# Two channels in one Toeplitz matmul, and filter rows loaded in pieces on 13, 11 or 9 DMA engines

## The chip, the core and the metric

The kernel runs on one core of one Trainium2 chip. The metric is the device time of one execution in microseconds; the time of before is the median of three runs, and one further execution was profiled.

## What is computed

Two independent blocks, whose outputs are put side by side (512 columns each, 2048 positions, bf16).

```python
# block A: attention, 32 heads of 16
qkv = (x @ wqkv).reshape(B, S, 3, H, Dh).transpose(2, 0, 3, 1, 4)
p = softmax(einsum("bhqd,bhkd->bhqk", q, k) * Dh ** -0.5)
a = einsum("bhqk,bhkd->bhqd", p, v).transpose(0, 2, 1, 3).reshape(B, S, D) @ wo
# block B: gated long convolution, 512 channels
k_shift = sum(k shifted by t * shift_k[:, ks - 1 - t])      # 4 taps
kv = k_shift * v
y = irfft(rfft(kv, 2S) * rfft(ssm_k, 2S))[:S] + kv * ssm_D  # causal convolution over 2048 positions
b = q * y
out = concatenate([a, b], -1)
```

## The kernel before

All five engines run instruction lists that are written out in full when the program is built. A planner in the kernel keeps a modelled time for each engine (`Eng.op`, `Tensor.op`, `dma`) and places each piece of work into the list with it, so a change of any cost constant moves instructions everywhere.

**Attention.** There are 2048 blocks of 128 keys x 512 queries for one head. A step T (`emit_qk`, L681) multiplies two to four blocks (`qk_mm`, L728) into PSUM banks 0 to 5. ACT exponentiates most of them, two or three banks an instruction (`emit_exp`, L761). One block of some steps goes to DVE, which needs four instructions for it (`exp_on_dve`, L803, L810 twice, L815). Two steps later PE multiplies the results with V (`emit_pv`, L844). Projections of later head groups, the product with `wo` and the multiplies of the convolution's input are "units" (`pe_unit`, L438; `unit_step`, L1088) that are put between steps by due times (`jobs`, L1065). `warm_up` (L1202, matmuls at L1219) fills idle time of PE with matmuls by zeros.

**Convolution.** It runs on PE between the steps. For each channel the reversed filter row, with 128 zeros behind it, is stored in an HBM scratch `kz` (L553). A load (`load_wr`, L990) reads it 128 times, each partition shifted by one element: a Toeplitz matrix of 128 x 2048 in the ring `WR`. `WR` holds 16 rows: four slots of four channels; the last slot first holds parts of v (`VST`, L282). `conv_lags` (L1003) multiplies for each of 16 lags n and four channels c: weights are the input `KV[:, qd, n:16, c]` (128 positions x up to 16 blocks of positions, one block a column), the moving side is 128 columns of `WR`, and the four channels write four 32-row strips of PSUM bank 7. After four such groups (16 channels) DVE copies the bank to one half of `YB` (L1028), and after eight `conv_turn` (L1033) transposes eight 128x128 tiles back and DVE multiplies them into `QN`, which holds q (L1048). `KV` is written by DVE at L514, from the shift's matmuls (L468) times v. From step N_OPEN on the convolution runs (`emit_bg`, L1143): it takes up to seven lags between steps (`LAGS`), if the rows are expected to be there (`h_wr` + WAIT), if there is room before the next exponential, and if PE's instruction fetch is expected to keep up.

**Instruction fetch in the planner.** `Tensor.op` (L182) counts two instruction words for each matmul, in blocks of 256. Crossing into a block starts a fetch of the next that is taken to land FETCH (L108, 6.3 us) later; `spare` (L204) says how many words may still be issued, and `emit_bg` (L1169) and `warm_up` (L1215) keep to it.

**Queues.** Filter rows go out on SP's queue, each group of four loads waiting for the last matmul that read its slot. POOL's queue carries the copies into `QT` (L499), the loads and stores of `QN` (L1000, L1052), and the stores of `OUTA` (L966). POOL starts with memsets (L392 to L403) and builds diagonal matrices of the taps (L560).

Of the kernel before, what the change touches and what calls it, by code (L numbers as in the profile page):

```python
# [9 lines left out]
U16 = mybir.dt.uint16  # L10

# [13 lines left out]
NB = S // 128  # L25
PAD = 128
# [3 lines left out]
R_W = 16  # L30
# [6 lines left out]
N_OPEN = 66  # L37
# [34 lines left out]
PLAN = 710  # L72
# [13 lines left out]
DMA_KB = 394  # L86
X_KB = 200
WINDOW = 3.4
HALF = 0.25
TURN = 0.2  # L90
# [17 lines left out]
FETCH = 6.3  # L108
# [111 lines left out]
def bass_concat_heads__mha_block__ssm_conv_h3__prompt_kernel(  # L220
# [36 lines left out]
    KV = sb("KV", [128, C // 4, NB, 4])  # L257
# [143 lines left out]
    h_va1 = pool.op(lambda e: e.memset(VA[:, :, :, 8 * VW:VROW].rearrange("p s k e -> p (s k) e"), 1.0))  # L401
    h_qt0 = pool.op(lambda e: e.memset(QT[:, 1:R_Q, :, :].rearrange("p r n f -> p (r n f)"), 0.0), us=(1.5, 1.6))
# [87 lines left out]
    def evac_unit(u, bank, h):  # L490
# [18 lines left out]
        elif kind == "kv":  # L509
            _, c, i = u  # L510
            dst = KV[:, 32 * c:32 * c + 32, NB - 4 - 4 * i:NB - 4 * i, :]
            val = VST[c][:, NB - 4 - 4 * i:NB - 4 * i, :].rearrange("p b (k c) -> p k b c", c=4)
            src = PS[:, bank, :].rearrange("p (b k c) -> p k b c", b=4, c=4)
            h_kvc[c] = hh = urgent(lambda e: e.tensor_tensor(dst, src, val, ALU.mult), [h, h_vn[c]], us=V512)  # L514
# [470 lines left out]
    h_yb = [None]  # L985
# [4 lines left out]
    def load_wr():  # L990
        while wr_free and wr_next[0] < C // 4:
            (i, dep), qd = wr_free.pop(0), wr_next[0]
            wr_next[0] += 1
            wr_slot[qd] = i
            for c in range(4):
                src = bass.AP(tensor=kz_ap.tensor, offset=kz_ap[4 * qd + c, 0].offset, ap=[[1, 128], [1, S]])
                h_wr[qd] = dma(sp, d_wr[i], WR[:, 4 * i + c, :], src, [h_kzw[0], dep])
# [4 lines left out]

    def conv_lags(qd, n0, n1):  # L1003
        kk = qd % 8
        deps = [h_wr[qd], h_kvc[qd // 32]]
        r = 4 * wr_slot[qd]
        if kk % 4 == 0 and n0 == 0:
            deps.append(bank_free[BGB])

        def fn(e):  # L1010
            ins = None
            for n in range(n0, n1):
                for c in range(4):
                    ins = e.matmul(PS[32 * c:32 * c + NB - n, BGB, 128 * (kk % 4):128 * (kk % 4) + 128],  # L1014
                                   lhsT=KV[:, qd, n:NB, c],
                                   rhs=WR[:, r + c, 128 * (NB - 1 - n):128 * (NB - n)],
                                   start=(n == 0), stop=(n == NB - 1), tile_position=(0, 32 * c))
            return ins
        h = pe.op(fn, deps, run=LAG * (n1 - n0), kind="C", lat=0.4)
        if n1 == NB:  # L1020
            wr_free.append((wr_slot[qd], h))
            load_wr()
            if kk % 4 == 3:
                half = kk // 4
# [4 lines left out]
                            [h, h_yb[0]], slack=S_C, us=V512)  # L1029
# [3 lines left out]
    def conv_turn(b, bank):  # L1033
        pbf = PS[:, bank, :].bitcast(BF16)

        def fn(e):
            ins = None
            for k in range(8):
                ins = e.transpose(pbf[:, 128 * k:128 * k + 128], YB[:, k // 4, 128 * (k % 4):128 * (k % 4) + 128],
                                  IDN[:, :])  # L1040
            return ins
        h = pe.op(fn, [bank_free[bank], h_ybw[0], h_idn], run=0.445, kind="F")
        h_yb[0] = h
        sl = b // 8
        yv = pbf.rearrange("p (c j) -> p c j", j=32)[:, :, 0:NB].rearrange("p c j -> p j c")
        yv = bass.AP(tensor=yv.tensor, offset=pbf[:, NB - 1:NB].offset, ap=[yv.ap[0], [-1, NB], [32, CHB]])
        qv = QN[:, :, CHB * (b % 8):CHB * (b % 8) + CHB]
# [11 lines left out]
    units = [("kv", c, i) for c in range(2) for i in range(4)] + [(x, 1, i) for i in range(4) for x in "kv"]  # L1059
# [7 lines left out]
    jobs += [(step(9 + 7 * c) - 8, ("kv", c + 2, i)) for c in range(2) for i in range(4)]  # L1067
    jobs += [(step(25 + 2 * qb) + 8 * t, ("op", qb, t)) for qb in range(NQB - 1) for t in range(4)]
    jobs.sort(key=lambda j: j[0])
    state = {"qd": 0, "lag": 0, "turn": False, "started": False, "lags": 0.0, "left": C // 4 * NB, "t": 0.0}  # L1070
# [6 lines left out]
    def next_unit(T):  # L1077
        if T < N_OPEN:
            return early[0] if early and ready(early[0][1]) else None
        if state["turn"]:  # L1080
            return T, ("turn", state["qd"] // 8 - 1)
# [6 lines left out]
    def unit_step(T):  # L1088
# [7 lines left out]
        while not tight:  # L1096
# [23 lines left out]
            us = pe.turn("F") + (0.445 if u[0] == "turn" else 0.478 if u[0] in ("kv", "v") else 2 * MM) + SWITCH  # L1120
# [22 lines left out]
    def emit_bg(T):  # L1143
# [5 lines left out]
        if T - end[0] in tail_mm:  # L1149
            assert st["qd"] == C // 4 and not st["turn"], (T, st)  # L1150
# [3 lines left out]
        if st["qd"] == C // 4 and not st["turn"]:  # L1154
# [3 lines left out]
        if st["turn"] and st["qd"] == C // 4:  # L1158
# [11 lines left out]
        while left > 0 and st["qd"] < wr_next[0] and kv_n[st["qd"] // 32] == 4 and at(h_wr[st["qd"]]) + WAIT <= pe.t:  # L1170
            if st["turn"] and st["qd"] % 4 == 3 and st["lag"] + left >= NB:
                left = NB - 1 - st["lag"]
                if left <= 0:
                    break
# [3 lines left out]
            n1 = min(n0 + left, NB)  # L1178
# [4 lines left out]
            st["lag"] = n1 % NB  # L1183
            if n1 == NB:
                st["qd"] += 1
                if st["qd"] % 4 == 0:
                    st["turn"] = st["turn"] or st["qd"] % 8 == 0
                    break

    def filler_place(limit):  # L1190
# [5 lines left out]
        if state["started"] and state["lag"]:  # L1196
            return BGB, 0, NB, 128 * (state["qd"] % 4), 1, False
# [53 lines left out]
    assert state["qd"] == C // 4 and not state["turn"] and not jobs and not part[0], (state, jobs)  # L1251
# [65 lines left out]
```

## Time and profile before

| | |
|---|---|
| runs shown | 826.47 us median (825.16, 826.47, 830.9) |
| the profiled execution | 828.52 us, its span 826.8 us |
| PE clock granted, mean | 0.996 |
| first and last convolution matmul starts | 89.7 and 804.1 us |
| filter loads | 512 of 512 KB, 8.4 us from issue to landing (median) |
| DMA packets | 109235, 291.41 MB, mean 352 GB/s |
| ACT busy by windows | 99.4% from 100 to 200 us, 96.8% from 200 to 300, 99.3% from 300 to 400, 99.9% or more from 400 to 700 |
| DMA engines' busy share | 0.98 to 1.03 from 100 to 780 us |

Busy time is the time in which an engine had at least one instruction in execution; ACT's instructions overlap at their ends, so their mean duration times their number is more than the busy time. The chain of waits gives ACT's exponentials (L761) 77.2% of the span, four DVE lines 10%, PE lines 9%. POOL and SP have nothing on it after the first 11 us. A row of a group reads: line, engine, operation, output <- inputs, shapes, count, then busy us, mean ns, and the engine's idle time ahead of it with what ended it.

### The profile page before, as it was taken

The numbers are of one execution on the slowest core, as the hardware profiler recorded it, in microseconds if no ns is written. First come the engines' busy times: TensorE is split into PE (matmuls) and PEld (weight loads), VectorE is DVE, ScalarE is ACT, GpSimd is POOL, SyncE is SP. The second block draws the span as 40 slices with busy tenths as digits, with TensorE's granted clock in tenths as the row PEclk, the third lists the DMA queues.
The fourth block names the chain that finished last, engine by engine and source line by source line (L and its number), as shares of the span: only waits on it lengthen the run. The fifth ranks groups of instructions, "written<-read, shape, count | busy, mean of one in ns | idle before, by whom it ended". The sixth has DMA issues, their size and how long they took to land.

```text
span 826.8 us, 30549 instructions
## 1 busy us (share of the span) xinstructions
PE 762.2 (92%) x13603; PEld 324.2 (39%) x13642; DVE 794.2 (96%) x1360; ACT 807.0 (98%) x727; POOL 78.7 (10%) x155
## 2 busy tenths in 40 slices
PE   8998989999999899999899999999999999998987
PEld 3343434443333344444333344444433333333332
DVE  4999999999999899999999999999999999999985
ACT  6999999999999899999999999999999999999987
POOL 3300320010100101001011010101002002010000
PEclk9999999999999999999999999999999999999999
DMA  9998499999999999999999899999999999999922
GB/s 220 233 300 304 151 382 404 385 379 407 393 407 405 394 401 389 405 354 367 394 388 391 318 372 383 394 408 387 408 407 352 378 393 362 399 382 367 375 83 77
DMA packets 109235, 291.41 MB, mean 352 GB/s; under 512 B 37680, under 2 KB 41648, under 8 KB 108720
## 3 DMA queue, kind: packets, MB, share of 16 engines
q1 hardware_dynamic: 102256, 280.80, 90.8%
q0 software_dynamic: 5648, 8.27, 3.1%
q8 instruction: 108, 1.77, 0.9%
q10 hardware_dynamic: 1200, 0.39, 0.2%
q14 instruction: 23, 0.19, 0.1%
HBM read 276.83 MB, written 6.42 MB: 343 GB/s over the span
## 4 chain that ended last, share of the span: by engine, by line
ACT 77%; DVE 10%; PE 9%; issue 2%; DMA 1%; SPq 0%
ACT PT L761 77%; DVE EH L810 4%; PE PS L728 3%; DVE FX L803 2%; PE PS L1014 2%; PE PS L844 2%; DVE PTD L815 2%; PE PS L1219 1%; PE PS L468 1%; DMA xT<-in_A_x_dram 1%; DVE DT L905 0%; DVE YB L1028 0%; SPq L312 0%; DVE KV L514 0%; DVE OTN L925 0%
## 5 line engine op out<-in xcount | busy, mean ns | idle before, releaser
L761 ACT ACTIVATE PT<-PS 128x1024 bf16<-128x1024 f32 (+2 forms) x722 | 804.1, 1376 | 8.8 <-PE PS L728 8.3
L728 PE MATMUL PS<-QT,KTo 32*128 32x512 bf16 x2048 | 287.1, 385 | 38.7 <-ACT PT L761 14.1
L844 PE MATMUL PS<-PT,VA 128*32 128x512 bf16 x1771 | 199.7, 391 | 6.6 <-issue 3.5
L1014 PE MATMUL PS<-WR,KV 128*12 128x128 bf16 (+15 forms) x8192 | 201.6, 220 | 4.4 <-issue 4.3
L803 DVE TENSOR_SCALAR FX<-PS 128x512 f32<-128x512 f32 x277 | 187.9, 682 | 8.3 <-PE PS L728 8.0
L815 DVE SCALAR_TENSOR_TENSOR PTD<-EH,FX 128x512 uint16<-128x512 f32 x277 | 185.7, 677 | 0.0
L810 DVE SCALAR_TENSOR_TENSOR EH<-EH 128x512 f32<-128x512 f32 x277 | 185.4, 680 | 0.0
L810 DVE SCALAR_TENSOR_TENSOR EH<-FX 128x512 f32<-128x512 uint16 x277 | 184.5, 682 | 0.1
L1014 PEld LDWEIGHTS PS<-WR,KV 128*12 128x12 bf16 (+15 forms) x8192 | 140.6, 88 | 71.9 <-issue 42.5
L728 PEld LDWEIGHTS PS<-QT,KTo 32*128 32x128 bf16 x2048 | 73.3, 91 | 237.8 <-ACT PT L761 178.9
L1219 PE MATMUL PS<-IDN,ZW 128*32 128x512 bf16 (+3 forms) x498 | 132.2, 334 | 0.0
L312 POOL DMA_DIRECT2D QT<-QS x120 | 59.2, 501 | 483.7 <-DVE DR L912 133.7
L844 PEld LDWEIGHTS PS<-PT,VA 128*32 128x32 bf16 x1771 | 48.0, 93 | 114.0 <-issue 97.5
L844 PE MATMUL PS<-PTD,VA 128*32 128x512 bf16 x277 | 83.1, 383 | 0.0
L1219 PEld LDWEIGHTS PS<-IDN,ZW 128*32 128x32 bf16 x498 | 41.8, 96 | 24.1 <-issue 10.4
L905 DVE STREAM_TRANSPOSE DT<-PS 128x512 f32<-128x512 f32 x32 | 22.7, 709 | 7.3 <-PE PS L844 6.8
L1028 DVE CAST YB<-PS 128x512 bf16<-128x512 f32 x32 | 21.9, 684 | 1.4 <-PE PS L1219 1.1
L844 PEld LDWEIGHTS PS<-PTD,VA 128*32 128x32 bf16 x277 | 20.4, 95 | 1.6 <-DVE PTD L815 0.2
L955 PE MATMUL PS<-WKV,OTN 128*128 128x512 bf16 x53 | 16.9, 383 | 2.1 <-issue 1.6
L479 PE MATMUL PS<-WKV,xT 128*128 128x128 bf16 x256 | 18.1, 220 | 0.1
L456 PE MATMUL PS<-xT,WKV 128*128 128x512 bf16 (+1 forms) x52 | 15.0, 373 | 2.9 <-issue 1.1
L447 PE MATMUL PS<-xT,WQ 128*128 128x512 bf16 x45 | 14.4, 382 | 2.4 <-issue 2.1
(65 smaller groups left out, 209.2 us busy)
## 6 DMA issues: line engine op xcount, KB each, us to landing
WR<-kz_scratch SPq DMA_DIRECT2D x512, 512.0 KB, 8.4
kz_scratch<-WR SPq DMA_DIRECT2D x1, 2176.0 KB, 8.3
QN<-in_B_q_dram POOLq DMA_DIRECT2D x2, 1024.0 KB, 12.4
out_dram<-QN POOLq DMA_DIRECT2D x2, 1024.0 KB, 8.6
QT<-QS POOLq DMA_DIRECT2D x120, 16.0 KB, 5.3
out_dram<-OUTA POOLq DMA_DIRECT2D x12, 128.0 KB, 5.2
QN<-in_B_ssm_k_dram SPq DMA_DIRECT2D x1, 1024.0 KB, 8.3
OTN<-in_B_ssm_k_dram SPq DMA_DIRECT2D x1, 1024.0 KB, 9.2
```

Of the source, the lines that this page charges most:

```text
L312: f(outp, inp).then_inc(dsem.sem, 16)
L479: ins = e.matmul(PS[:, bank, 128 * j:128 * j + 128], lhsT=xT[:, dc, (4 * sc + j) * 128:(4 * sc + j + 1) * 128], rhs=WV[:, dc, o * 128:(o + ...
L728: ins = e.matmul(PS[:, bank, :], lhsT=KTo[32 * s:32 * s + 32, OF[n_] % 2, kt * 128:(kt + 1) * 128], rhs=QT[32 * s:32 * s + 32, n_ // 2 % R ...
L761: h_exp[T] = act.op(lambda e: e.activation(PT[:, p0:p0 + n, :].rearrange("p b f -> p (b f)"), PS[:, banks[0]:banks[0] + n, :].rearrange("p ...
L803: h_f = urgent(lambda e: e.tensor_scalar(fx, PS[:, bank, :], FIX_ADD, FIX_HI, ALU.add, ALU.min), [h, h_last.get(i - R_FX)], slack=S_FX)
L810: st["h"] = dve.op(lambda e: e.scalar_tensor_tensor(eh, src, (P1, P2)[j], src, ALU.add, ALU.mult), [st["h"], h_last.get(i - R_EH)], us=us)
L815: lambda e: e.scalar_tensor_tensor(out16, eh, P3, fx, ALU.mult, ALU.add),
L844: ins = e.matmul(dst, lhsT=w, rhs=rhs, start=(k == 0), stop=(k == KT - 1), tile_position=(0, 32 * s))
L905: h_t = urgent(lambda e: e.transpose(out=dt, in_=PS[:, PVB, :]), [h, h_mul.get(n - 1)], slack=S_T, us=(0.63, 0.751))
L1014: ins = e.matmul(PS[32 * c:32 * c + NB - n, BGB, 128 * (kk % 4):128 * (kk % 4) + 128], lhsT=KV[:, qd, n:NB, c], rhs=WR[:, r + c, 128 * (NB ...
L1028: hh = urgent(lambda e: e.tensor_copy(YB[:, half, :].rearrange("p (k i) -> p k i", k=4), src), [h, h_yb[0]], slack=S_C, us=V512)
L1219: pe.op(lambda e, s=s, k=k, rhs=rhs, bank=bank, rows=rows, c0=c0, first=first: e.matmul(PS[32 * s:32 * s + rows, bank, c0:c0 + 128 * k], l ...
```

## The change

The convolution is cut otherwise. Filters are loaded as Toeplitz matrices of 64 partitions instead of 128, and two channels lie above each other in the 128 partitions. The input `KV` becomes twice as large, [128, 64, 2, 32, 4]: blocks of 64 positions, where the column of an upper channel has zeros in the lower half and the other way round. POOL sets it to zero once. A group `qd` is eight channels, there are 64 groups, and 32 lags of 64 positions instead of 16 of 128; the number of matmuls is the same, 8192, with 2 to 32 weight columns. Lag -1 is a half step with 64 moving columns. One `conv_turn` is due after four groups, with four transposes instead of eight.

Rows: each half's 64 shifted rows of four channels come in two DMAs, of 52 and 12, then 55 and 9, then 63 and 1 rows; the division changes at groups 21 and 43. By the change's name these run on 13, 11 and 9 of the 16 DMA engines. `WR` has three slots of four rows instead of four. The multiplies of chunk 1 of `KV` become units behind the start of the convolution, and N_OPEN goes from 66 to 64. The planner's constants for the plan's length (710 to 705), for turns (0.2 to 0.05) and for the instruction fetch (6.3 to 5.5 us) change, and the rates of the row loads are given (260 and 215 KB/us).

```diff
-R_W = 16
+R_W = 12
-N_OPEN = 66
+N_OPEN = 64
+KV1 = 2
-PLAN = 710
+PLAN = 705
+PARTS = [(52, 12), (55, 9), (63, 1)]
+PHASE = [21, 43]
+RATES = [260, 215]
-TURN = 0.2
+TURN = 0.05
-FETCH = 6.3
+FETCH = 5.5
...
-    KV = sb("KV", [128, C // 4, NB, 4])
+    KV = sb("KV", [128, C // 8, 2, 2 * NB, 4])
...
+    h_kv0 = pool.op(lambda e: e.memset(KV[:, :, :, :, :].rearrange("p o r u g -> p (o r u g)").bitcast(U32), 0), us=(8.8, 8.9))
     h_qt0 = pool.op(lambda e: e.memset(QT[:, 1:R_Q, :, :].rearrange("p r n f -> p (r n f)"), 0.0), us=(1.5, 1.6))
...
-            h_kvc[c] = hh = urgent(lambda e: e.tensor_tensor(dst, src, val, ALU.mult), [h, h_vn[c]], us=V512)
+            for half in range(2):
+                for ch in range(2):
+                    hs, cs = slice(64 * half, 64 * half + 64), slice(64 * ch, 64 * ch + 64)
+                    dst = KV[cs, 16 * c:16 * c + 16, 1 - half, q0 + ch:q0 + 8:2, :].rearrange("p o q g -> p q o g")
+                    h_kvc[c] = hh = (dve.op if half or ch else urgent)(
+                        lambda e, dst=dst, hs=hs, ch=ch: e.tensor_tensor(dst, src[hs, :, ch], val[hs, :, ch], ALU.mult),
+                        [h, h_vn[c], h_kv0], us=(0.335, 0.46))
...
-            for c in range(4):
-                src = bass.AP(tensor=kz_ap.tensor, offset=kz_ap[4 * qd + c, 0].offset, ap=[[1, 128], [1, S]])
-                h_wr[qd] = dma(sp, d_wr[i], WR[:, 4 * i + c, :], src, [h_kzw[0], dep])
+            parts = PARTS[sum(qd >= q for q in PHASE)]
+            for ch in range(2):
+                p0 = 0
+                for n in parts:
+                    row = 128 * (qd // 16) + 64 * ch + 4 * (qd % 16)
+                    src = bass.AP(tensor=kz_ap.tensor, offset=kz_ap[row, p0].offset, ap=[[1, n], [LKZ, 4], [1, S]])
+                    h_wr[qd] = dma(sp, d_wr[i], WR[64 * ch + p0:64 * ch + p0 + n, 4 * i:4 * i + 4, :], src,
+                                   [h_kzw[0], dep], kb=16 * n, rate=RATES[len(parts) - 2 + (parts[0] == 63)])
+                    p0 += n
...
-            for n in range(n0, n1):
-                for c in range(4):
-                    ins = e.matmul(PS[32 * c:32 * c + NB - n, BGB, 128 * (kk % 4):128 * (kk % 4) + 128],
-                                   lhsT=KV[:, qd, n:NB, c],
-                                   rhs=WR[:, r + c, 128 * (NB - 1 - n):128 * (NB - n)],
-                                   start=(n == 0), stop=(n == NB - 1), tile_position=(0, 32 * c))
+            for n in range(n0, n1):
+                d = DIST[n]
+                w = 64 if d < 0 else 128
+                for g in range(4):
+                    kv = KV[:, qd, (1 + d) % 2, (1 + d) // 2 * 2:2 * NB, g]
+                    ins = e.matmul(PS[32 * g:32 * g + 2 * ((30 - d) // 2 + 1), BGB, 128 * kk:128 * kk + w],
+                                   lhsT=kv, rhs=WR[:, r + g, S - 64 * d - 128:S - 64 * d - 128 + w],
+                                   start=(n == 0), stop=(n == NLAG - 1), tile_position=(0, 32 * g))
...
-            for k in range(8):
-                ins = e.transpose(pbf[:, 128 * k:128 * k + 128], YB[:, k // 4, 128 * (k % 4):128 * (k % 4) + 128],
-                                  IDN[:, :])
+            for k in range(4):
+                ins = e.transpose(pbf[:, 128 * k:128 * k + 128], YB[:, b % 2, 128 * k:128 * k + 128], IDN[:, :])
...
-    units = [("kv", c, i) for c in range(2) for i in range(4)] + [(x, 1, i) for i in range(4) for x in "kv"]
+    units = [("kv", 0, i) for i in range(4)] + [(x, 1, i) for i in range(4) for x in "kv"]
...
+    jobs += [(N_OPEN + KV1 + 4 * i, ("kv", 1, i)) for i in range(4)]
```

## The prediction

> **What bounds the kernel now.** I read the page first (busy shares, slices, queues), then the groups by form, then ACT's waits, then the timeline around those waits.
>
> ```profile
> PE 762.2 (92%) x13603; PEld 324.2 (39%) x13642; DVE 794.2 (96%) x1360; ACT 807.0 (98%) x727; POOL 78.7 (10%) x155
> ```
>
> ACT is busy 98% and DVE 96%: the 2048 blocks of the exponential are divided between them, 1771 on ACT and 277 on DVE (four DVE instructions each). PE's 92% counts pipelined matmuls and is no bound by itself. The groups by form price ACT's work:
>
> ```profile
> L761 ACT ACTIVATE PT<-PS 128x1536 bf16<-128x1536 f32 x321 | 493.9, 1605 | 6.5 <-PE PS L728 6.0
> L761 ACT ACTIVATE PT<-PS 128x1024 bf16<-128x1024 f32 x398 | 429.0, 1188 | 1.0 <-PE PS L728 1.0
> ```
>
> A third block in an instruction costs 1605 - 1188 = 417 ns, so 1771 blocks are 738.5 us of the 804.1 us busy at L761; the other 65.6 us over 722 instructions is 0.091 us each. ACT idles little between 60 and 815 us, and only for PE:
>
> ```profile
> ACT PT L761 <- PE PS L728: 7.0, 10, 2.1
> ```
>
> What holds PE then is not a semaphore. In the timeline, 28 convolution matmuls that belong to one step stop after the first, and ACT starves a step later; near the end the same happens ahead of L844:
>
> ```profile
> 222.41 0.22 PE L1014 MATMUL PS<-WR,KV 128*9 128x128 bf16 x1
> ...
> 223.82 0.57 PE L1014 MATMUL PS<-WR,KV 128*9 128x128 bf16 x27 [1.19 <-issue]
> ...
> 224.75 5.62 ACT L761 ACTIVATE PT<-PS 128x1536 bf16<-128x1536 f32 x5 [0.46 <-PE PS L728]
> ```
> ```profile
> 789.23 0.40 PE L844 MATMUL PS<-PT,VA 128*32 128x512 bf16 x3 [1.98 <-issue]
> ```
>
> "issue" inside a run of equal matmuls means that PE had no instruction. The queues show who brings them, and what it shares the DMA engines with:
>
> ```profile
> q1 hardware_dynamic: 102256, 280.80, 90.8%
> ...
> q8 instruction: 108, 1.77, 0.9%
> ```
>
> 108 packets for 13642 pairs of weight load and matmul: 126 pairs a packet. In the trace's packet records of q8 a packet takes about 1.08 us; at the seven longest stalls (0.6 to 2.0 us, at 105, 223, 229, 278, 355, 649 and 787 us) PE goes on 1.3 to 1.6 us after a packet's end, and after the first six the next packet starts 3.8 to 5.1 us later. I read that as a request at the moment PE enters a new block of instructions: about 3.8 + 1.1 + 1.4 = 6.3 us from request to use. After the stall at 787 us the filter loads have just ended (DMA share 0.27 from 789.2 to 791.1 us) and the next packet starts after 1.8 us: 4.3 us in all. So about 2 us of each fetch is waiting behind filter rows. From 100 to 795 us the packets come 7.15 us apart on average, and 28 of 97 spacings are under 6.3 us: this is close to a bound.
>
> By the Trainium skill (DMA: Bandwidth & Descriptors, section Queues, rings and completion order) an engine drains a packet of 9 to 17 descriptors of one ring before it turns to the next ring; with the 159 ns that a 4096-byte row takes here that would be 1.4 to 2.7 us, and the 2 us above agree.
>
> **The change part by part.** The sum is made against the profiled execution: 828.52 us, of which the span is 826.8. The median of the runs shown, 826.47, lies 2.05 lower.
>
> *ACT.* Counted in the two built programs: 722 instructions at L761 become 727, and 1771 blocks become 1774. 5 x 0.091 + 3 x 0.417 = +1.7 us, on the bounding engine, so on the path.
>
> *DVE.* The 16 multiplies into KV (L514, 0.60 us apart when back to back in the chain) become 64 on 64 partitions x 256 elements. No such row exists; 0.60 each is the upper end (+28.8 us), and the nearest rows, 128x256 at L916 (415 ns against 685 for 512 columns at L1048) and L504 (425 ns), say 0.27 us less than a full one: 0.33 x 64 = 21 us, +11.5. I take that. The 32 copies to YB (L1028) become 16: -9.6. Three fewer blocks at L803 to L815: -12 x 0.60 = -7.2. Together -5 us; at the upper end +12. DVE is 96% busy but the order leaves it queues several blocks deep, so I count 0; at the upper end most of the excess falls on the 8 multiplies' windows in mid-run, and up to +3 could show. The first four units of chunk 1 move behind the start of the convolution, past matmuls that need only chunk 0: 0.
>
> *PE.* The convolution stays 8192 matmuls (256 of them 64 columns wide instead of 128), with 2 to 32 weight columns instead of 1 to 16: the load's mean goes from 83 ns (1 column) to 94 (15), 96 for the 32-column loads at L1219, hidden beside the matmuls (PEld 39%). 64 fewer transposes at L1039, 8 in 0.45 us: -3.6 us of PE. Fillers at L1219 go from 498 to 511, keep-busy matmuls from 2 to 22. All together 13611 pairs instead of 13642, still about 107 fetches. PE is not the bound: 0.
>
> *POOL.* A new memset of KV, 8192 words a partition, ahead of those of QT and WR. L402 takes 1.79 us for 2048 bf16: 7.2 us by elements, 14.4 by bytes. L560 behind it starts at 15.28 us today and would slip by 0 to 5 us; its result is first used at 44.28 us (chain, L468): 0. The first copies to QT on the same queue go out at 30.14: 0.
>
> *SP and the filter rows.* 512 loads of 512 KB become 256 of pieces, 2 MB for each 8 channels instead of 4: 134 MB instead of 268. The filter's part of q1's 90.8% is 268/281 of it, 86.8%, and halves to 43%. That the pieces run on 13, 11 and 9 engines is what the change says of itself, and 52 = 13 x 4, 55 = 11 x 5, 63 = 9 x 7 fit it; no trace of before shows it. At 159 ns a row of 4 KB (median of q1's packets of that size), the busiest engine has 40 rows per 8 channels on 13 engines (6.4 us), 48 on 11 (7.6), and 58 on 9 (9.2). The convolution uses 8 channels' rows in (804 - 89.5) / 64 = 11.2 us on average, and three slots hold 34 us of them. SP issues 4 DMAs per 11 us instead of 8, at 0.43 us. So rows are in time: 0 on the path, with the 9-engine third closest. The third slot holds VST until chunk 1 is multiplied, so it fills late; the two before it hold 22 us of work: 0.
>
> The Trainium skill speaks against this part (DMA: Bandwidth & Descriptors, section Rules for kernel authors): two transfers to disjoint partition halves gain nothing over one of 128 partitions, and the outermost dimension should be a multiple of 16 so that all 16 engines work. By that rule the loads only get slower; by the rows above they remain shorter than their use, so the sum would be the same by both, unless the last third is late (the third rival below).
>
> *Instruction fetches.* The fetch of PE's instructions now finds less ahead of it, and the order is written for it: FETCH, the latency that the order keeps clear of, goes from 6.3 to 5.5 us, so matmuls may stand closer. The latency lies between 4.3 us (nothing ahead) and 6.3 (as now). Rows take half the time of the 16 engines, so I take the middle, 5.3, 0.2 under the 5.5 of the order; before, 6.3 stood against 6.3. Of ACT's 7.0 us of waits between 0 and all 7.0 stay; I take 2.0 left, for fetches that still meet a full engine: -5.0.
>
> **Sum:** 828.5 + 1.7 - 5.0 = 825.2 us for a run like the profiled one, 823.2 by the median of the runs.
>
> **The rivals.** All by the median of the runs.
>
> 1. All fetches are free: the 7.0 us go, and PE's granted clock no longer falls behind a stall (0.66 to 0.72 from 789 to 795 us), about 1 to 3 us more. 826.5 + 1.7 - 7.0 = 821.2, down to 818. For it: half the rows. Against it: each busy engine is as full as before while it works.
>
> 2. The other side: the fetch gains nothing where it counts, while the order has moved the matmuls closer. 28 blocks stand at the order's limit; if as many stand at 5.5 us and the fetch takes 6.2 when it meets a loaded engine, each loses 0.7 us: 9.8 us with half of them loaded, 19.6 with all. Against today's 7.0 that is 826.5 + 1.7 + 2.8 = 831, to 841. It decides from about 27% of those 28 blocks (5.3 us lost, the 7.0 less 1.7). For it: the 1.4 us after the packet and the 1.1 us in it don't shrink. Against it: the wait ahead of it is the only part that load sets.
>
> 3. Rows late in the last third: if a row takes over 11.2 us / 58 = 193 ns on 9 engines, PE waits in a convolution step and QK of the next step waits behind it. At 198 ns (the slowest twentieth of today's rows) that is 0.3 us for each of 21 loads: +6 us, 834.
>
> 4. Nothing changes but the work: stalls as today, 826.5 + 1.7 = 828.2 (826 to 829.5).
>
> **How the numbers follow.** Forecast (820.5 to 826) 0.50, rival 1 0.15, rival 4 0.17, rival 2 0.13, rival 3 0.05. The time is the forecast's, 823.2. The range 818.5 to 831 leaves out about a third of rival 1 and most of 2 and 3, some 0.2 together. A measurement of this kernel can tell about 1% from no change, 818.2 to 834.7 here: below it only the best end of rival 1 (0.05), above it the worse part of 2 and 3 (0.08), between 0.87.
>
> **What would show it.** ACT at L774: 727 instructions, busy near 805.8. ACT's waits for QK between 60 and 815 us: 2 us instead of 7.0 (0 for rival 1, 10 or more for rival 2). "issue" gaps over 0.6 us in PE: fewer than seven; spacings of q8 packets down to about 5.3. Rows: filter share near 43%, no PE wait on WR's DMA in the last third. KV multiplies near 0.33 us apart, DVE busy 789 us. What would make it wrong: a fetch that waits as long as now, or rows slower than 193 ns.

## The result

The changed kernel takes 975.87 us (median of four runs, 955.62 to 998.33) against 827.17 us before (825.16 to 830.9): a ratio of 1.162, 95% interval 1.148 to 1.176. It is slower by 16.2%, 134 us of 827, far outside the predicted range of 818.5 to 831 us. Two of the four, the profiled one of 998.33 us among them, ran over 1.5% longer than the fastest and are left out of the ratio, so shares of the loss are taken from ratios, and the profile only tells how the loss of its own execution is made up.

### The profile page after: what moved, and what is told of

The parts are those of the page before. It is cut to its first block, busy times and chain, and to the rows that moved or that the text cites. A ratio compares the mean times of both kernels' runs of the same rounds, so it can differ in the third digit from the quotient of the medians.

```text
span 996.6 us, 30275 instructions
## 1 busy us (share of the span) xinstructions
PE 834.2 (84%) x13611; PEld 345.4 (35%) x13611; DVE 803.5 (81%) x1380; ACT 823.4 (83%) x732; POOL 85.5 (9%) x156
## 3 DMA queue, kind: packets, MB, share of 16 engines
q1 hardware_dynamic: 63772, 146.56, 59.4%
## 4 chain that ended last, share of the span: by engine, by line
DMA 37%; ACT 25%; PE 22%; DVE 10%; issue 3%; SPq 2%; DVEq 0%
DMA WR<-kz_scratch 36%; ACT PT L774 24%; PE PS L741 7%; PE PS L1038 6%; PE PS L857 4%; DVE EH L823 3%; SPq L318 2%; PE PS L1241 2%; DVE FX L816 2%; DVE PTD L828 2%; DVE KV L526 1%; PE PS L463 1%; PE PS L454 1%; DVE DT L918 0%; DMA xT<-in_A_x_dram 0%
## 5 line engine op out<-in xcount | busy, mean ns | idle before, releaser
L774 ACT ACTIVATE PT<-PS 128x1024 bf16<-128x1024 f32 (+2 forms) x727 | 820.4, 1282 | 161.9 <-PE PS L741 160.7
L741 PE MATMUL PS<-QT,KTo 32*128 32x512 bf16 x2048 | 308.8, 412 | 33.1 <-issue 9.1
L1038 PE MATMUL PS<-WR,KV 128*26 128x128 bf16 (+8 forms) x8192 | 244.6, 234 | 106.0 <-DMA WR<-kz_scratch 84.4
L1038 PEld LDWEIGHTS PS<-WR,KV 128*18 128x18 bf16 (+7 forms) x8192 | 163.4, 100 | 203.3 <-DMA WR<-kz_scratch 91.0
L857 PE MATMUL PS<-PT,VA 128*32 128x512 bf16 x1774 | 210.2, 414 | 8.5 <-DVE DT L918 5.1
L1241 PE MATMUL PS<-IDN,ZW 128*32 128x512 bf16 (+3 forms) x511 | 140.5, 350 | 0.2
L857 PEld LDWEIGHTS PS<-PT,VA 128*32 128x32 bf16 x1774 | 47.9, 94 | 129.5 <-issue 110.4
L857 PE MATMUL PS<-PTD,VA 128*32 128x512 bf16 x274 | 87.6, 413 | 1.9 <-DVE PTD L828 1.9
L463 PE MATMUL PS<-xT,WKV 128*128 128x512 bf16 (+1 forms) x64 | 21.2, 435 | 1.1 <-DVE KV L526 0.6
L857 PEld LDWEIGHTS PS<-PTD,VA 128*32 128x32 bf16 x274 | 20.8, 97 | 3.7 <-DVE PTD L828 2.4
L511 DVE CAST KTo<-PS 128x512 bf16<-128x512 f32 (+1 forms) x16 | 10.7, 670 | 13.6 <-PE PS L463 13.6
L454 PE MATMUL PS<-xT,WQ 128*128 128x512 bf16 x60 | 19.2, 416 | 0.0
```

Source lines behind the costliest of these rows:

```text
L454: return e.matmul(PS[:, bank, :], lhsT=WQ[:, dc, o * 128:(o + 1) * 128], rhs=xT[:, dc, qb * 512:(qb + 1) * 512], start=(dc == 0), stop=(dc ...
L463: return e.matmul(PS[:, bank, c0:512], lhsT=WK[:, dc, o * 128:(o + 1) * 128], rhs=xT[:, dc, sc * 512 + c0:(sc + 1) * 512], start=(dc == 0) ...
L741: ins = e.matmul(PS[:, bank, :], lhsT=KTo[32 * s:32 * s + 32, OF[n_] % 2, kt * 128:(kt + 1) * 128], rhs=QT[32 * s:32 * s + 32, n_ // 2 % R ...
L774: h_exp[T] = act.op(lambda e: e.activation(PT[:, p0:p0 + n, :].rearrange("p b f -> p (b f)"), PS[:, banks[0]:banks[0] + n, :].rearrange("p ...
L857: ins = e.matmul(dst, lhsT=w, rhs=rhs, start=(k == 0), stop=(k == KT - 1), tile_position=(0, 32 * s))
L1038: ins = e.matmul(PS[32 * g:32 * g + 2 * ((30 - d) // 2 + 1), BGB, 128 * kk:128 * kk + w], lhsT=kv, rhs=WR[:, r + g, S - 64 * d - 128:S - 6 ...
```

## The profile after

The first line of the page's busy shares, then ACT's groups by form and its wait for PE over the whole span, and the two queues.

```profile
PE 834.2 (84%) x13611; PEld 345.4 (35%) x13611; DVE 803.5 (81%) x1380; ACT 823.4 (83%) x732; POOL 85.5 (9%) x156
```
```profile
L774 ACT ACTIVATE PT<-PS 128x1536 bf16<-128x1536 f32 x314 | 465.2, 1523 | 69.8 <-PE PS L741 68.9
L774 ACT ACTIVATE PT<-PS 128x1024 bf16<-128x1024 f32 x410 | 422.9, 1092 | 91.0 <-PE PS L741 90.7
```
```profile
ACT PT L774 <- PE PS L741: 160.7, 136, 6.5
```
```profile
q1 hardware_dynamic: 63772, 146.56, 59.4%
...
q8 instruction: 107, 1.75, 0.8%
```

ACT does the same work, and its share falls from 98% to 83%, because it stands 160.7 us, at 136 places, for PE's QK matmuls. Before, the same wait was 8.3 us over the whole span:

```profile
ACT PT L761 <- PE PS L728: 8.3, 12, 2.1
```

That is +152.4 of the +169.8 us between the two profiled spans. Another 16.4 us is ACT's busy time, 823.4 against 807.0: instructions that start after a wait no longer overlap the one before. So the question is what stops PE. PE's waits, the costliest:

```profile
PE PS L1038 <- DMA WR<-kz_scratch: 84.4, 29, 6.3
PE PS L1038 <- issue: 21.4, 14, 5.5
PE PS L741 <- issue: 9.1, 3, 3.4
```

Two causes stand side by side. 84.4 us are waits for filter rows, of which before had none; they stand in every third of the convolution (25.4 us from 60 to 350 us, 39.8 to 650, 19.2 after it). 30.5 us and a few more are waits for instructions ("issue": PE waited for nothing that the profile shows). All 15 of these gaps over 0.6 us lie at word 192 or 193 of a block of 256 instruction words, when each weight load, matmul and semaphore wait of PE counts as one word, and so do the six of before. The first kind in the timeline of all engines: the first matmuls of a new group of rows start 5.57 us late, the QK behind them as well, and ACT starves.

```profile
419.36 0.89 PE L1038 MATMUL PS<-WR,KV 128*32 128x128 bf16 x28 [5.57 <-DMA WR<-kz_scratch]
...
420.18 0.61 PE L741 MATMUL PS<-QT,KTo 32*128 32x512 bf16 x3
...
420.84 1.02 ACT L774 ACTIVATE PT<-PS 128x1024 bf16<-128x1024 f32 x1 [5.23 <-PE PS L741]
```

The second kind, the answer to the stall shown of before in the middle of 28 equal matmuls; here it takes 5.46 us where that one took 1.19:

```profile
230.08 0.57 PE L1038 MATMUL PS<-WR,KV 128*18 128x128 bf16 x25
236.11 0.28 PE L1038 MATMUL PS<-WR,KV 128*12 128x128 bf16 x3 [5.46 <-issue]
...
236.76 0.61 PE L741 MATMUL PS<-QT,KTo 32*128 32x512 bf16 x3
...
241.06 0.39 PE L741 MATMUL PS<-QT,KTo 32*128 32x512 bf16 x3
```

Ahead of L857 (L844 before), where the second stall of before lay, one of 1.01 us stands at 311 us:

```profile
311.23 0.40 PE L857 MATMUL PS<-PT,VA 128*32 128x512 bf16 x4 [1.01 <-issue]
```

Look also at the durations. After most long stops a matmul of 512 columns takes 0.61 us instead of 0.39 for some microseconds, so PE, which was no bound, is late again. The windows of the three thirds (us, then busy us of PE and its instructions, the granted clock, the DMA share, GB/s):

```profile
100.00:350.00 250.00, 191.55 (x3566) 0.85 0.82 173
350.00:650.00 300.00, 243.16 (x4442) 0.87 0.70 172
650.00:815.00 165.00, 144.67 (x2519) 0.92 0.58 176
```

The granted clock was 0.99 to 1.00 in these stretches before. And 172 to 176 GB/s is about half of the 331 to 395 GB/s of before, the same figure with 13, 11 and 9 engines. By itself that does not tell what sets the rate, for the kernel also asks for half the bytes; the time of a single row does.

The trace's packet records, one a row of 4 KB on one engine, say what a row takes and how many rows are under way at once (the most frequent number):

| stretch | rows under way, after | median row, after | median row, before |
|---|---|---|---|
| 100 to 200 us | 13 | 312 ns | 159 ns |
| 200 to 300 us | 13 | 305 ns | 161 ns |
| 400 to 500 us | 11 | 266 ns | 160 ns |
| 500 to 600 us | 11 | 255 ns | 160 ns |
| 700 to 800 us | 9 | 199 ns | 159 ns |

So the pieces do run on 13, 11 and 9 engines, and a row takes up to twice as long as the 159 ns that the prediction carried over. Rows under way x 4096 bytes / median row is 171 GB/s at 13 engines, 169 at 11 (400 to 500 us) and 185 at 9: the fewer engines write, the quicker each row, and the sum hardly moves. That hints at something other than the number of engines.

## The experiments

**The theories.** A: a load whose rows go to only 64 of the 128 partitions is slow, because the engines share the ways into those partitions. A', its sharper form, put up after run 5: a row keeps to 159 ns only if each engine has a way of its own, which needs 128 partitions and all 16 engines. Against A: the rows are slow because too few engines work (B), because the matmuls' closer order is late itself (C), or because of the form of the transfer (four rows far apart for each partition). F: the loss is instruction fetches that come later than the order of the matmuls has them. K: the four narrow multiplies into KV in a row hold PE up. A ratio below is to runs of before on the same chip, with its 95% interval.

**1. Full-height loads.** The changed kernel with its order of matmuls untouched, but the rows loaded as 128 partitions (the lower halves then hold the upper channels' rows, so half of the convolution is not the reference's).

```diff
-            for ch in range(2):
-                p0 = 0
-                for n in parts:
...
+            for g in range(4):
+                row = 128 * (qd // 16) + 4 * (qd % 16) + g
+                src = bass.AP(tensor=kz_ap.tensor, offset=kz_ap[row, 0].offset, ap=[[1, 128], [1, S]])
+                h_wr[qd] = dma(sp, d_wr[i], WR[:, 4 * i + g, :], src, [h_kzw[0], dep], kb=512, ...)
```

> The changed kernel, its order on every compute engine the same, but each group's 2 MB come as four loads of 128 partitions (one channel's 128 shifted rows each) instead of four pieces of 64-partition halves. The lower halves so hold the upper channel's rows again, and half of the convolution is not the reference's. Theory A (a transfer whose rows go to 64 partitions moves its rows at half the pace; in the changed kernel's trace a 4 KB row took 312 ns in the median from 100 to 200 us, 159 before): rows back to about 160 ns, no wait of PE for rows, time 822 to 830. Theory B (too few engines, with 13 in the first third): rows also in time here, since these loads run as before's do, 822 to 830; B and A part in the next two runs. Theory C (the rows are late only as a consequence, and the closer order of matmuls and its instruction fetches is the cause): still slower than 900.

Measured: 845.95 us, 1.022 (1.019 to 1.026). The median row takes 159 ns again, and no wait of PE for rows is left. ACT's wait and the first of PE's:

```profile
ACT PT L774 <- PE PS L741: 20.2, 37, 2.3
```
```profile
PE PS L1037 <- issue: 9.7, 10, 2.6
PE PS L741 <- ACT PT L774: 6.5, 27, 0.5
PE PS L857 <- DVE DT L918: 5.3, 10, 1.3
PE PS L741 <- DVE KV L526: 3.8, 7, 1.0
```

The rows are back as A and B had it, though the time is 16 us above the range that both gave; C, over 900, is out. What follows: with the same bytes and the same order, 14.0 of the 16.2% (115 of 134 us) go when the loads reach all partitions on all 16 engines. This edit changes both at once; runs 2 and 5 change one of the two each. What is left, 2.2% or 18 us, is another matter (runs 8 to 10).

**2. 64 rows in one piece.** Halves as in the changed kernel, but on 16 engines.

```diff
-PARTS = [(52, 12), (55, 9), (63, 1)]
+PARTS = [(64,), (64,), (64,)]
```

> The changed kernel with each half in one piece of 64 rows (twice as few DMAs, the same bytes), order of PE the same. Theory A (64 partitions): still late, rows of 4 KB at about 318 ns (16 engines in place of 8 engines' worth of reach, 2 x 159), time 930 to 1000. Theory B (engines missing): all engines work, rows back near 160 ns, time 822 to 840. Theory C: over 900.

Measured: 976.34 us, 1.180 (1.176 to 1.184). The median row takes 316 to 318 ns in every stretch, twice the 159 ns, with 16 rows under way: 16 x 4096 / 318 = 206 GB/s at most, as A had it. B, rows near 160 ns with all engines at work, is out as the sole cause. There is no wait for rows any more; instruction fetches stop PE instead:

```profile
PE PS L1038 <- issue: 72.2, 31, 6.0
PE PS L741 <- issue: 12.8, 7, 3.3
PE PS L857 <- issue: 9.7, 4, 4.2
```

The Trainium skill states a cause that would give this (SBUF — State Buffer, section Door 1: The DMA port swizzle): partitions 0 to 63 reach 8 of 16 ports, a bound of about 218 GB/s by its figures. The 206 GB/s here agree; the records name no port, so the sharing itself is not seen.

**3. Nine engines throughout.**

```diff
-PARTS = [(52, 12), (55, 9), (63, 1)]
+PARTS = [(63, 1), (63, 1), (63, 1)]
```

> The changed kernel with pieces of 63 and 1 rows for all groups, order of PE the same. Theory A: a row takes about 165 ns as in the last third of the changed kernel (9 engines on 8 engines' worth of reach), the total pace is the same 220 GB/s or a little over what 13 engines gave, so the first two thirds get faster: 870 to 940. Theory B (more engines are better): slower than the changed kernel, over 990, since the first third then has 9 engines instead of 13.

Measured: 1028.47 us, 1.228 (1.218 to 1.238). Nine rows are under way, the median row takes 179 to 255 ns by stretch, and the mean 211 to 259, above the 193 ns that rows on 9 engines may take. A's forecast failed here: it had rows of 165 ns and 870 to 940 us, and the time came out where B put it, over 990. So with halves the number of engines matters as well. PE's waits are the mirror image of the run before: all rows, hardly a fetch.

```profile
PE PS L1038 <- DMA WR<-kz_scratch: 152.8, 40, 8.5
PE PS L741 <- ACT PT L774: 5.9, 24, 0.5
```

Runs 2 and 3 show the two ends: with 16 engines the rows are in time and the fetches are late (8 to 9 us from the entry into a block of instructions to use, about 3 with 9 engines); with 9 the rows are late. The 13, 11 and 9 engines lie between, pay some of both, and at 1.162 lose less than either end.

**4. The kernel before, its loads in halves.**

```diff
-                src = bass.AP(tensor=kz_ap.tensor, offset=kz_ap[4 * qd + c, 0].offset, ap=[[1, 128], [1, S]])
-                h_wr[qd] = dma(sp, d_wr[i], WR[:, 4 * i + c, :], src, [h_kzw[0], dep])
+                for p0 in (0, 64):
+                    src = bass.AP(tensor=kz_ap.tensor, offset=kz_ap[4 * qd + c, p0].offset, ap=[[1, 64], [1, S]])
+                    h_wr[qd] = dma(sp, d_wr[i], WR[p0:p0 + 64, 4 * i + c, :], src, [h_kzw[0], dep], kb=256)
```

> The kernel before with each load of 128 partitions cut in two loads of 64 partitions, 256 KB each; same bytes, same 128 shifted rows, order of all compute engines the same, 16 engines. Theory A: 8 engines' worth of reach for 268 MB at 200 to 220 GB/s is 1220 to 1340 us for the rows alone: time 1250 to 1450. Theories B and C: as before, 826 to 835, with the issue on SP (8 x 0.43 us in 5.6 us) still ahead of need.

Measured: 1101.35 us (two runs, 1085 and 1117, no interval), with these waits for rows:

```profile
PE PS L1015 <- DMA WR<-kz_scratch: 185.0, 82, 4.8
```

Halves hurt the old kernel too, so the two-channel form is not the cause. But the size was wrong: the median row takes 194 to 282 ns and the rows come at 237 to 329 GB/s, more than 206. Upper and lower half alternate here every 256 KB; if each engine can be at another place of the queue, both halves are written at once for part of the time. That would explain it; the records do not tell which half a row goes to.

**5. Full height on 11 and 9 engines.** Run 1 with its 128 partitions in pieces of 99, 27, 1 and 1.

```diff
-            for g in range(4):
-                row = 128 * (qd // 16) + 4 * (qd % 16) + g
...
+            p0, row = 0, 128 * (qd // 16) + 4 * (qd % 16)
+            for n in (99, 27, 1, 1):
+                src = bass.AP(tensor=kz_ap.tensor, offset=kz_ap[row, p0].offset, ap=[[1, n], [LKZ, 4], [1, S]])
```

> The run with loads of 128 partitions, its order of PE the same (FETCH 5.5), but the rows in pieces of 99, 27, 1 and 1 partitions for four channels at once, so that the large pieces work on 11 and 9 engines. Theory F2 (the requests for instructions go round eight engines, and those numbered above the filter's are free: in the changed kernel six of eight requests in turn waited 5 to 8 us while its rows went on 13 engines, two or three of eight with 11, two with 9): half of the requests wait about 1 us, the stalls halve, ACT waits 8 to 13 us instead of 20, time 832 to 840. Rival (every request waits for whatever traffic there is): as before that change, 846, or slower since the rows use the engines longer.

Measured: 924.57 us, 1.117 (1.112 to 1.121). The expectation failed, and F2 stays untested, for the rows were late:

```profile
PE PS L1036 <- DMA WR<-kz_scratch: 61.4, 18, 6.1
```

They take 208 and 256 ns (median) from 100 to 300 us although the pieces lie over both halves. So theory A as first put is too narrow. A' was made to cover this: 11 engines that each write nine neighbouring partitions may have no fixed way of their own and meet on some. But from 300 us on the median is 159 to 171 ns and the mean (194 to 212) no more than in run 1 (197 to 204), which A' does not explain; what then remains is that at least 48 rows (9 x 4 and 3 x 4) on the busiest engine at 212 ns, 10.2 us, leave little of the 11.2 us that a group may take. A' is not shown.

**6. Four rows of each partition in one DMA.** Run 1 with one load of 2 MB in place of four of 512 KB.

```diff
-            for g in range(4):
-                row = 128 * (qd // 16) + 4 * (qd % 16) + g
-                src = bass.AP(tensor=kz_ap.tensor, offset=kz_ap[row, 0].offset, ap=[[1, 128], [1, S]])
...
+            row = 128 * (qd // 16) + 4 * (qd % 16)
+            src = bass.AP(tensor=kz_ap.tensor, offset=kz_ap[row, 0].offset, ap=[[1, 128], [LKZ, 4], [1, S]])
+            h_wr[qd] = dma(sp, d_wr[i], WR[:, 4 * i:4 * i + 4, :], src, ..., kb=2048, ...)
```

> The full-height loads (128 partitions on all 16 engines, the same bytes; the lower halves of the multiplies read other rows, so half of the convolution's products are not the reference's), but four rows of each partition in one DMA of 2 MB instead of four DMAs of 512 KB. Theory A' (a row is slow only where the engines share their way into the partitions, as they do when a transfer reaches 64 partitions or runs on fewer engines than 16): rows of 159 to 200 ns and a time of 840 to 855 us, as the full-height loads in four DMAs (846). Rival (the changed kernel's form of transfer, four rows far apart behind one another for each partition, is slow by itself, whatever the partitions): rows of 250 ns or more and 900 us or more.

Measured: 862.36 us, 1.042 (1.038 to 1.046). The median row takes 159 ns, the mean 184 to 187: the form of the transfer is not what slows the rows. The time is 16 us above run 1 and above the range that A' gave; PE's waits for instructions at the convolution are 14.8 us instead of 9.7. Why is open.

**7a. The halves on two queues.** Full result: 64 rows in one piece, the upper halves on SP's queue, the lower on POOL's.

```diff
+    d_wp = [DmaSem(sem(f"d_wp{i}")) for i in range(R_W // 4)]
...
-                    h_wr[qd] = dma(sp, d_wr[i], WR[64 * ch + p0:64 * ch + p0 + n, 4 * i:4 * i + 4, :], src,
+                    (h_wr, h_wp)[ch][qd] = dma((sp, pool)[ch], (d_wr, d_wp)[ch][i], WR[...], src,
```

> The changed kernel with each half in one piece of 64 rows, the upper half from SP's queue, the lower from POOL's; nothing is left out, order of PE the same. Theory A (one transfer reaches half of the partitions' ports, and the queue works its transfers off one after the other): both halves are in flight together, rows of 4 KB fall from 318 towards 160 to 220 ns, time 845 to 880, with fetches waiting as in the run of 128 partitions. Rival (64-partition transfers are slow in themselves, or POOL's queue is too slow for 64 of them): still over 930.

Measured: 924.41 us, 1.116 (1.112 to 1.121), between A's range and the rival's. The median row of SP's queue takes 258 to 307 ns from 100 to 800 us, against 318 in run 2: a second queue helps only in part.

**7b. The halves in turn.** Full result: eight DMAs of 256 KB a group, upper and lower half alternating, as in run 4.

```diff
+            for g in range(4):
+                for ch in range(2):
+                    row = 128 * (qd // 16) + 64 * ch + 4 * (qd % 16) + g
+                    src = bass.AP(tensor=kz_ap.tensor, offset=kz_ap[row, 0].offset, ap=[[1, 64], [1, S]])
+                    h_wr[qd] = dma(sp, d_wr[i], WR[64 * ch:64 * ch + 64, 4 * i + g, :], src, ..., kb=256, ...)
```

> The changed kernel with all its results, its group of rows loaded by eight DMAs of 256 KB, upper and lower half in turn, each on 16 engines. Theory A' (two transfers that stand behind one another in the queue and go to different halves overlap in part): rows between 200 and 275 ns, as the loads of before cut into halves had (199 to 273), against a need of 11.2 us for each group of 512 rows, which 16 engines meet up to 350 ns a row: rows in time, instruction fetches in part late, 860 to 940 us. Rival (a half is a half, the order of the DMAs does not matter): rows of 318 ns, 970 to 985 us, as with 64 rows in one piece (976).

Measured: 870.71 us, 1.055 (1.051 to 1.059), at the low end of what A' gave. The median row takes 266 to 278 ns, and no wait of PE for rows is left:

```profile
ACT PT L774 <- PE PS L741: 39.4, 49, 3.4
```
```profile
PE PS L1036 <- issue: 18.0, 13, 3.3
```

The order and the cut of the DMAs, with 16 engines, take back 10.7 of the 16.2%. It is the best form of the two-channel kernel found here that computes everything, and still 5.5% behind the kernel before.

**8. A longer fetch allowance on the full-height loads.**

```diff
-FETCH = 5.5
+FETCH = 6.3
```

> The run with loads of 128 partitions (lower halves hold the upper channel's rows, so half of the convolution is not the reference's), with FETCH back at 6.3, so that the order keeps matmuls as far apart as before. Theory F (what was left of that run, 846 against 828, is PE waiting for blocks of instructions that the order expected 5.5 us after the request, while a tenth of them took over 6.5): ACT's waits fall from 20 to 5 to 8 us, time 828 to 834. Rival (the larger KV, the four multiplies into it and the 64-column steps cost it): 840 to 848, waits of ACT unchanged.

Measured: 844.93 us, 1.021 (1.018 to 1.024): no gain that these intervals can tell; F fails for the 18 us, as far as the planner's allowance can show it. PE's waits for instructions at the convolution fall from 9.7 to 5.9 us, but ACT's wait for PE stays at 20.3 us. In run 1, PE's waits for the KV multiplies (4.3 us) outweigh those for instructions (2.0 at the convolution) from 40 to 170 us; from 170 to 400 us it is the other way round (1.5 and 9.4). The timeline of run 1 has a place of the first kind, where PE waits for the last of four multiplies that stand one behind another on DVE:

```profile
112.24 0.39 PE L741 MATMUL PS<-QT,KTo 32*128 32x512 bf16 x3 [1.03 <-DVE KV L526]
```

**9 and 10. One wide multiply, and the longer allowance again.** The four multiplies of a unit of KV as one of 128 x 512, then also FETCH = 6.3.

```diff
-            for half in range(2):
-                for ch in range(2):
...
+            dst = KV[:, 16 * c:16 * c + 16, 1, q0:q0 + 8, :].rearrange("p o (b h) g -> p b h o g", h=2)
+            h_kvc[c] = hh = urgent(lambda e: e.tensor_tensor(dst, src, val, ALU.mult), [h, h_vn[c], h_kv0], us=V512)
```

> The full-height loads (846 us; half of the convolution's products are not the reference's), and in place of the four multiplies of 64 partitions by 256 for each unit of KV one of 128 by 512, as before the change had (KV then holds other values than the reference's in half of its places). Theory K (of the 19 us that the full-height loads are above before, the four multiplies, 4 x 0.44 us in a row in front of PE's next step, make about half): 834 to 840 us, ScalarE's wait for PE down from 20 us to 8 to 12 us. Rival (all of the 19 us is instruction fetches that come later than the order has them): 844 to 848 us, ScalarE's wait unchanged.

> The run before with one more edit: the order of the work is planned with 6.3 us for an instruction fetch in place of 5.5 us. Theory K with late fetches (the rest of the distance is fetches that come late by the order): 827 to 834 us, and no wait of PE for instructions over 3 us in total. Rival (the fetches that are late cost nothing that a longer allowance gives back, as with the four narrow multiplies, where it gave 1 us): the same as the run before within 2 us.

Measured: 835.62 us, 1.008 (1.005 to 1.012), and 831.6 us, 1.007 (1.004 to 1.010). ACT's wait falls from 20.2 to 8.6 us, near the 8.3 of before:

```profile
ACT PT L769 <- PE PS L736: 8.6, 15, 1.2
```

The time fits K: the wide form takes back 1.4% of the time, about 11.6 us. But with other times for the multiplies, and with another allowance, the planner also puts the matmuls in another order (13571 weight loads in run 9, 13611 in run 1), so the 1.4% is of both together. The longer allowance gives nothing that these intervals can tell, so the rival of run 10 holds, although PE's waits at the convolution for instructions fall from 6.3 to 3.0 us. The last 0.7% (5.6 us) was not divided further; 1.7 us of it is ACT's larger work by the sum on record, which no run here measures by itself.

**11. The kernel before with the planner counting semaphore waits as instruction words.** In the built program the fetch stalls of before and after stand at the same place of a block of 256 words, once the waits that PE executes are counted; the planner leaves them out.

```diff
+        words += max(len(self.ops[-1][0]) - 1, 0)
```

> The kernel before with one line added: the planner's count of PE's instruction words also counts the extra wait instructions that an operation with several semaphores needs (331 to 335 over the program), which it left out. In before's trace the seven long stalls all stand at the same word of a block of 256 once these are counted, and 300 words off by the end where the planner expects it. Theory F: the planner then keeps its distance at the right places, ACT's 7.0 us of waits fall to 1 to 4, time 3 to 6 us shorter, 821 to 825. Rival (the place does not matter, only the average pace): no difference within 1.5 us.

Measured: 827.09 us, 1.000 (0.997 to 1.003). The rival holds. One gap for instructions of 2.2 us is left of the six over 0.6 us, but ACT's wait for PE is 8.9 us against 8.3, and nothing is gained; the line also makes the planner order the work anew.

## Why the prediction was wrong

By its own steps:

- **SP and the filter rows: this step failed.** It says "At 159 ns a row of 4 KB", and from it 6.4, 7.6 and 9.2 us a group against a need of 11.2 us. The engines were counted rightly (13, 11 and 9 rows under way), but the 159 ns belong to loads of 128 partitions. With the mean row of each third as measured (322 ns at 100 to 200 us, 268 at 400 to 500, 220 at 700 to 800) the busiest engine needs 40 x 322 = 12.9 us, 48 x 268 = 12.9 and 58 x 220 = 12.8 us: late in every third, not only in the last. The waits for rows bear it out: 25.4, 39.8 and 19.2 us by thirds. Runs 1 and 2 show it directly, both on 16 engines: 159 ns with 128 partitions, 318 with 64. So q1's share of the engines' time came down only to 59.4%, where the filter's was to be near 43%.
- **The weighing of the rule** went wrong at the same point. The Trainium skill's rule (DMA: Bandwidth & Descriptors, section Rules for kernel authors) is that two transfers to disjoint partition halves gain nothing over one of 128 partitions. The prediction found that the loads "remain shorter than their use" all the same; that judgement used the 159 ns again.
- **Rival 3** had the mechanism, slow rows that hold PE, and its threshold of 193 ns (run 3 passes it with a mean row of 211 to 259 ns). Its price was bounded by "the slowest twentieth of today's rows", 198 ns. That is no bound, for every row of before went to 128 partitions. It gave +6 us and a chance of 0.05. Rival 2's mechanism, fetches that come late, took part as well, at about 9 us where it had 6.2.
- **Instruction fetches: this step failed too, and depends on the first.** Forecast: latency down from 6.3 to 5.3 us, since "Rows take half the time of the 16 engines". Worked out from the packet records as the prediction did, from the entry into a block to use, the median was about 6 us before and about 9 us after from 200 to 350 us; then, with fewer engines in use, about 4 us (350 to 640) and 3.4 us (640 to 800). In run 2 it is 8 to 9 us. In run 1, with half the bytes in rows of 159 ns, it is 4.7: there the wait does get shorter, as forecast. In the changed kernel a row took twice as long, and half the rows then take as much time as before. Instead of fewer than seven gaps over 0.6 us there are 15, of 30.6 us in all.
- **DVE.** A narrow multiply takes 422 ns (median) and the next one starts 0.45 us after it, not 0.33 us: 64 x 0.45 - 16 x 0.60 = +19.2 us instead of +11.5. A wide one takes 684 ns but lets the next instruction start after 0.60 us; the narrow ones do not overlap at all, with 0.03 us between them. More important, counting the multiplies at 0 because DVE's queue is deep was wrong: four stand in a row, 1.78 us, in front of PE's next need. Runs 1 and 9 put the price, the planner's new order included, at about 11.6 us, beyond the +3 that the prediction allowed.

```profile
L526 DVE TENSOR_TENSOR KV<-PS,WR x32: 406/422/429, 43.5 to 119.9; 64x256 bf16<-64x256 f32 x32
```
```profile
L514 DVE TENSOR_TENSOR KV<-PS,WR x8: 627/684/684, 43.5 to 64.1; 128x512 bf16<-128x512 f32 x8
```
```profile
102.96 1.78 DVE L526 TENSOR_TENSOR KV<-PS,WR 64x256 bf16<-64x256 f32 x4
```

The first row is of the changed kernel, the second of before, the third of run 1.

- **ACT.** 727 instructions at L774 as counted; they are busy 820.4 us instead of 805.8, because 136 waits break the overlap.
- **PE.** The amount of work was right. That it "is not the bound" held only at the full clock: after a long stop a matmul of 512 columns takes 0.61 us instead of 0.39. The trace has some 30 stretches of more than 1.5 us with slow matmuls, about 150 us together, against at most four, of 10 us, before.
- **POOL.** The memset (6.9 us) is hidden, as forecast.

The sum of the causes, in ratios: of the 16.2%, 14.0 go with loads of 64 partitions on fewer engines in place of 128 on 16 (run 1; they show as late rows, late fetches and slow matmuls behind stops), 1.4 with the narrow multiplies and the order made for them (run 9), 0.8 is not settled. The 14.0 do not divide further: halves alone, on all 16 engines, cost 18.0% (17.6 to 18.4), full height on 11 and 9 engines 11.7%, and the change with its 13, 11 and 9 engines 16.2% (14.8 to 17.6). So against halves on 16 engines, choosing the engines gives back about 1.8 points, and the two intervals touch.

## What to carry to other kernels

A duration from the trace holds for the shape it was measured on: before a DMA row's time is carried to a new transfer, ask which partitions it reaches and on how many engines, for bytes halved at half the rate save nothing. Where an in-order engine needs both data and instructions through the same DMA engines, taking engines from one to spare the other moved the stop here, as runs 2 and 3 show, and did not remove it. And an engine at 92% whose clock falls after long stops is a bound as soon as there are such stops.

## What the runs showed of the hardware

- Rows of 4 KB: 159 ns with 128 partitions on 16 engines, 316 to 318 ns with 64 partitions, 208 to 256 ns with all partitions on 11 engines from 100 to 300 us of run 5, but 159 to 171 ns from there on. Halves that alternate every 256 KB reached up to 329 GB/s in run 4, above the 206 GB/s of one half. The Trainium skill (SBUF — State Buffer, section "Can I just issue two DMAs to hit both halves?") gives 6% for two DMAs to the two halves; alternating loads that stand one behind another in a queue gain far more here, 329 against 206 GB/s.
- The fetch wait is uneven. Numbering the requests of the changed kernel's first third by eights, six of each eight mostly wait 4 to 11 us for their packet to start and the other two under 2 us; in run 3, with 9 engines in use, only two of eight wait long (2 to 6 us). This would fit fetches that go round eight engines, some of which carry rows; the records name no engine, so it is inferred, and run 5, made to try it, did not tell.
- Slow matmuls after a stop. Over the profiles of the changed kernel and of runs 2, 3 and 7b, of the stops of PE from 0.7 to 1.6 us 6 in 58 were followed, among the next six QK matmuls within 3 us, by one of over 0.55 us, of those from 1.6 to 2.5 us 19 in 35, and of the longer ones 66 in 70. The Trainium skill (TensorE: Matmul & The Clock Gate, Part 1) has half the clock after an idle window of about 3.4 us; here stops of 1.6 to 2.5 us already slow the matmuls more often than not, and in before's trace the granted clock is 0.50 from 791 to 793 us, behind the stop of 1.98 us.
